# Expert routing: the late tokens of an expert rounded to 64 rows instead of 128, and odd halves of two experts sharing a block

## The chip, the cores and the metric

One core of a Trainium2 chip runs the whole kernel in one launch. The metric is the device time in microseconds (us). TensorE (PE) multiplies, with a weight load (LDWEIGHTS, "PEld") ahead of each matmul; VectorE (DVE), ScalarE (ACT) and GpSimd (POOL) do the elementwise work; SyncE (SP) issues most DMAs, and POOL those that gather or scatter rows by an index.

## The reference, cut to what matters

Attention and a dense mixing layer (with a Fourier transform) make `x`, 8 x 576 = 4608 tokens of 512 channels. The last layer sends every token to one of 8 experts:

```
for b in range(B):
    for s in range(S):
        fresh_e = argmax(x[b, s] @ w_gate)
        e = fresh_e if s == 0 or local_gate[b, s] < 0.5 else prev_e
        prev_e = e
        h = maximum(x[b, s] @ w1[e], 0)          # 512 -> 1024
        out[b, s] = p[e] * (h @ w2[e])           # 1024 -> 512
```

With the inputs of `setup_inputs()` the reference sends 572, 576, 1884, 550, 466, 140, 399 and 21 tokens to experts 0 to 7; of the first four batches' tokens, 572, 0, 772, 9, 455, 125, 371 and 0.

## The kernel before, in words

Attention and the mixing layer take about the first 985 us. The expert stage, which the change touches, works in blocks of 128 tokens of one expert. `place` counts the tokens of each expert and gives each token a row in a block. It runs twice. The early call knows the first four batches only, and fills NEARLY = 9 blocks with whole 128s (four of expert 0, five of expert 2). The late call, when all logits are there, rounds what is left of each expert up to 128 rows: 60, 576, 1244, 550, 466, 140, 399 and 21 tokens make 1, 5, 10, 5, 4, 2, 4 and 1 blocks, 32 in all. Up to 34 are possible; 32 always run (`last_sure`), the last two stand behind branches on the count `used` (`rare`), and are left out with these inputs.

A block b is four steps. `load_x` gathers its 128 rows (POOL's indirect DMA) and turns them with a DMA transpose on SP's queue (xgt: channels on partitions). `e1` makes h: two groups fg of 512 hidden units, each a PSUM tile of 128 x 512 filled by 48 matmuls with a stationary 128x128 piece of w1 and the block's 128 tokens moving (three per pair, since weights and tokens are split in a high and a low f16 half: `PASS`). ACT's relu and one DVE instruction evict each group as the two f16 halves of hx. `e2` takes hx as stationary and w2 as moving operand: 24 matmuls of 512 columns. ACT scales the result (ys), and POOL scatters it to `out`. PE does `e1(b + 1)` before `e2(b)`, so an eviction has an `e2` to hide behind.

The weights of an expert are 2 MB for w1 and 2 MB for w2, each loaded in four pieces of 512 KB. They stand in three slots, and block b uses slot b % 3 (`RB`). `runs` orders the blocks so that those of one slot go through the experts in order, and a slot's expert changes seldom. `weights` issues every piece with a condition (`cond=c`): if the slot already holds the expert, the piece is skipped. A slot's w1 is free again after its own `e1`, and is needed two blocks and an `e2` later. SP issues in order, and each issue waits until the DMA issued eight before it has landed.

A scheduler orders the instructions of each engine, after the order in which they are written. Of two matmul streams that are open it may put pieces of one between pieces of the other. PE runs its list in order.

Of the kernel before, what the change touches and what calls it, by code (L numbers as in the profile page):

```python
# [24 lines left out]
NRARE = 2  # L25
# [4 lines left out]
def runs(n):  # L30

    size = [len(range(r, n, RB)) for r in range(RB)]
    return np.array([s // RB + sum(size[:s % RB]) for s in range(n)])
# [16 lines left out]
def prep(inputs):  # L50
# [105 lines left out]
    c32[:, 607:607 + NBLK - NEARLY] = np.r_[runs(NBLK - NEARLY - NRARE), NBLK - NEARLY - NRARE:NBLK - NEARLY][None, :]  # L156
# [32 lines left out]
def _build(tc, nc, ctx, A, stop):  # L189
# [65 lines left out]
    EB = cp.tile([1, NBLK], F32, name="EB")  # L255
    ebi = cp.tile([1, 2, NBLK], I32, name="ebi")
    used = cp.tile([1, 1], I32, name="used")
# [1039 lines left out]
    def place(nm, ncol, b0, nb, early, rp):  # L1297
# [11 lines left out]
        if ncol < 36:  # L1309
# [8 lines left out]
        nbk = rp.tile([128, 3, 8], F32, tag="nbk", name=f"nbk{nm}")  # L1318
        nc.vector.tensor_scalar(ni, cnt, 0.0 if early else 127.0, None, ALU.add)
        nc.vector.tensor_scalar(ni, ni, 7, None, ALU.arith_shift_right)  # L1320
        nc.vector.tensor_copy(nbk[:, 0], ni)
        nc.vector.tensor_tensor_scan(out=nbk[:, 1], data0=ones[:, 0:8], data1=nbk[:, 0], initial=0.0,
                                     op0=ALU.mult, op1=ALU.add)
        nc.vector.tensor_tensor(nbk[:, 2], nbk[:, 1], nbk[:, 0], op=ALU.subtract)
        if not early:
            nc.vector.tensor_copy(used, nbk[0:1, 1, 7:8])

        cmp = rp.tile([1, NBLK, 8], F32, tag="fs", name=f"cmp{nm}")
        nc.vector.tensor_tensor(cmp[:, :nb], nbk[0:1, 1].unsqueeze(1).to_broadcast([1, nb, 8]),
                                steps[0:1].unsqueeze(2).to_broadcast([1, nb, 8]), op=ALU.is_le)  # L1330
        nc.vector.tensor_reduce(EB[:, b0:b0 + nb], cmp[:, :nb], axis=AX.X, op=ALU.add)
        nc.vector.tensor_scalar(EB[:, b0:b0 + nb], EB[:, b0:b0 + nb], 7.0, None, ALU.min)
        nc.vector.tensor_copy(ebi[:, 0, b0:b0 + nb], EB[:, b0:b0 + nb])
        if b0 == 0:
            nc.vector.memset(ebi[:, 1, 0:RB], 1)
            nc.vector.tensor_tensor(ebi[:, 1, RB:nb], EB[:, RB:nb], EB[:, 0:nb - RB], op=ALU.not_equal)
        else:
            nc.vector.tensor_tensor(ebi[:, 1, b0:b0 + nb], EB[:, b0:b0 + nb], EB[:, b0 - RB:b0 + nb - RB],
                                    op=ALU.not_equal)
# [10 lines left out]
        ob = nbk[:, 2].unsqueeze(1).to_broadcast([128, ncol, 8])  # L1350
        pos = rp.tile([128, 36], F32, tag="pos", name=f"pos{nm}")[:, :ncol]
        if early:
            nc.vector.tensor_tensor(rvn, rvn, oh, op=ALU.mult)
            nc.vector.tensor_reduce(pos, rvn, axis=AX.X, op=ALU.add)
            lim = rp.tile([128, 36], F32, tag="lim", name=f"lim{nm}")[:, :ncol]
            nc.vector.tensor_tensor(rvn, nbk[:, 0].unsqueeze(1).to_broadcast([128, ncol, 8]), oh, op=ALU.mult)
# [102 lines left out]

    def weights(b, dst, src, k0, k1):  # L1460
# [5 lines left out]
        flat = dst[b % RB].rearrange("p c a n -> p (c a n)")  # L1466
        cols = slice(2048 * k0, 2048 * k1)
        nc.sync.dma_start(flat[:, cols], src[bass.ds(e, 1), :, cols].rearrange("o p x -> p (o x)"), cond=c)
# [7 lines left out]
    def e1(b, nxt=None):  # L1476

        ht = M["q"].tile([128, 2, 2, 512], F16, tag="hx", name=f"hx{b}", bufs=3)
        for fg in range(2):
            hp = (psM, psO)[fg].tile([128, 512], F32, tag="ho"[fg], name=f"ehp{b}_{fg}")  # L1480
            for f in range(4):
                n = 0
                cols = slice(128 * f, 128 * f + 128)
                for c in range(4):
                    for (x, y) in PASS:
                        nc.tensor.matmul(hp[:, cols], w1b[b % RB][:, 2 * c + fg, x, cols], xt[b][:, 4 * y + c],  # L1486
                                         start=n == 0, stop=n == 11, skip_group_check=True)
                        n += 1
                if f % 2 == 0 and nxt is not None:
                    load_w1(nxt, 2 * fg + f // 2, 2 * fg + f // 2 + 1)  # L1490
# [7 lines left out]
    def e2(b, nxt=None):  # L1498
        h = hb.pop(b)
        op = psO.tile([128, 512], F32, tag="o", name=f"eo{b}")  # L1500
        n = 0
        for f in range(8):
            for (x, y) in PASS:
                nc.tensor.matmul(op, h[:, f // 4, x, 128 * (f % 4):128 * (f % 4) + 128], w2b[b % RB][:, f, y],  # L1504
                                 start=n == 0, stop=n == 23)
                n += 1
            if f % 2 == 0 and nxt is not None:
                load_w2(nxt, f // 2, f // 2 + 1)
# [68 lines left out]
    e1(0, 2)  # L1577
    last_sure = NBLK - NRARE

    def sure(b):  # L1580
        return b if b < last_sure else None

    for b in range(last_sure):
        if b + RB == NEARLY:
            drain(r1)
        if sure(b + AHEAD) is not None:
            load_x(b + AHEAD)
        if b + 1 < last_sure:
            e1(b + 1, sure(b + RB))
        e2(b, sure(b + RB - 1))  # L1590


    nused = nc.values_load(used, min_val=0, max_val=NBLK - NEARLY)  # L1593

    def rare(b):
        if b == NBLK:
            return
        with tc.If(nused > b - NEARLY):
            load_x(b)
            load_w1(b)  # L1600
            load_w2(b)
            e1(b)
            e2(b)
            rare(b + 1)

    rare(last_sure)
# [17 lines left out]
```

## Time and profile before

| | us |
|---|---|
| three runs: lowest, median, highest | 1441.71, 1446.0, 1447.43 |
| the profiled execution: its time, its span | 1447.72, 1445.9 |
| PE busy | 1390.1 (96%) |
| mean granted TensorE clock | 0.985 |

The profile divides the span in instructions by line, engine and tile. A row with "x96" is 96 like instructions merged, with the first start and the time to the last end; a matmul's own duration holds its way through the array, so what one costs is read from start to start. Names lose their buffer numbers: w1b and w2b are the slots, hx the evicted h, ehp and eo the PSUM tiles of `e1` and `e2`.

### The profile page before, as it was taken

How to read it: one execution, taken by the hardware profiler on the slowest of the kernel's cores; microseconds unless marked ns; L12 is line 12 of the kernel's file. 1: busy time of each engine (PE TensorE's matmuls, PEld its weight loads, DVE VectorE, ACT ScalarE, POOL GpSimd, SP SyncE). 2: the span in 40 equal slices, each digit the busy share in tenths (PEclk: the TensorE clock that was granted, in tenths of full speed). 3: DMA queues.
4: the chain of work that ended last, by engine and by line, in shares of the span. 5: the costliest groups of instructions: out<-in, count | busy, mean ns of one | idle time of the engine just before them, and what ended most of it. 6: DMA issues, size and time to landing. Idle time of an engine off the chain costs nothing. (4 is left out here: it accounts for less than half of the span.)

```text
span 1445.9 us, 28499 instructions
## 1 busy us (share of the span) xinstructions
PE 1390.1 (96%) x11196; PEld 818.5 (57%) x11196; DVE 694.3 (48%) x1397; ACT 518.3 (36%) x953; POOL 382.3 (26%) x392
## 2 busy tenths in 40 slices
PE   7799999999999999999999999998999999999996
PEld 5554455454564544544544566446677776777774
DVE  5899856566625656656657563513821111111110
ACT  2543264455336445545446443111111111111111
POOL 1002243344324334334424332010121121212111
PEclk8999999999999999999999999999999999999998
DMA  6465294764469476476466454526939454962371
GB/s 258 161 221 178 89 261 118 194 202 129 125 162 246 126 191 188 118 194 199 112 184 175 141 132 128 190 68 183 255 82 288 89 145 124 290 202 76 90 237 43
DMA packets 221752, 238.29 MB, mean 165 GB/s; under 512 B 158703, under 2 KB 170095, under 8 KB 218928
## 3 DMA queue, kind: packets, MB, share of 16 engines
q1 hardware_dynamic: 215056, 216.25, 52.7%
q0 software_dynamic: 6560, 20.19, 4.4%
q8 instruction: 89, 1.46, 0.4%
q14 instruction: 47, 0.39, 0.1%
HBM read 268.31 MB, written 53.74 MB: 223 GB/s over the span
## 5 line engine op out<-in xcount | busy, mean ns | idle before, releaser
L1145 PE MATMUL acc<-w,ht 128*128 128x512 f16 x1728 | 409.5, 379 | 0.0
L1125 PE MATMUL hp<-ut,w 128*128 128x512 f16 x1536 | 365.6, 380 | 3.1 <-DMA ut<-unh 2.1
L1125 PEld LDWEIGHTS <-w 128*128 128x128 f16 x1920 | 182.9, 98 | 182.4 <-issue 10.7
L1145 PEld LDWEIGHTS <-ht 128*128 128x128 f16 x1728 | 165.6, 98 | 188.6 <-issue 8.6
L1486 PE MATMUL ehp<-xgt,w1b 128*128 128x128 f16 x3936 | 230.0, 220 | 2.5 <-DMA w1b<-WS 2.5
L1486 PEld LDWEIGHTS <-w1b 128*128 128x128 f16 x3936 | 224.6, 98 | 12.7 <-DMA w1b<-WS 2.8
L333 POOL TENSOR_TENSOR halfs<-stage,halfs 128x512 f16<-128x512 f32 x128 | 151.4, 1188 | 293.9 <-ACT halfs L332 274.5
L1504 PE MATMUL eo<-w2b,hx 128*128 128x512 f16 x984 | 222.2, 382 | 0.0
L1494 DVE SCALAR_TENSOR_TENSOR hx<-ehp,hx 128x512 f16<-128x512 f32 x82 | 56.6, 691 | 330.3 <-ACT hx L1493 330.3
L1133 DVE SCALAR_TENSOR_TENSOR ht<-hp,ht 128x512 f16<-128x512 f32 (+1 forms) x160 | 101.2, 633 | 158.1 <-ACT ht L1132 157.0
L1132 ACT ACTIVATE ht<-hp 128x512 f16<-128x512 f32 (+1 forms) x160 | 88.0, 550 | 231.9 <-PE hp L1125 231.7
L1504 PEld LDWEIGHTS <-hx 128*128 128x128 f16 x984 | 95.0, 98 | 107.2 <-issue 2.7
L1512 POOL DMA_INDIRECT out<-ys,sidx x41 | 42.0, 1023 | 324.0 <-ACT ys L1511 315.8
L1493 ACT ACTIVATE hx<-ehp 128x512 f16<-128x512 f32 x82 | 48.9, 597 | 178.7 <-PE ehp L1486 178.7
L1511 ACT ACTIVATE ys<-eo,scl 128x512 f32<-128x512 f32 x41 | 28.2, 687 | 184.0 <-PE eo L1504 184.0
L332 ACT CAST halfs<-stage 128x512 f16<-128x512 f32 x128 | 77.7, 615 | 9.5 <-DMA WS<-halfs 5.0
L331 ACT ACTIVATE stage<-stage 128x512 f32<-128x512 f32 x128 | 77.7, 623 | 0.2
L1454 POOL DMA_INDIRECT xg<-XS,gidx x41 | 42.4, 1033 | 126.1 <-DVE sidx L1421 50.9
L358 POOL TENSOR_TENSOR qh<-q,qh 128x1420 f16<-128x1420 f32 x12 | 34.6, 2884 | 53.2 <-ACT qh L357 53.1
L1125 PE MATMUL hp<-utr,w 128*128 128x256 f16 x384 | 47.1, 273 | 0.0
L570 PE MATMUL bp<-cst,eh 128*128 128x289 f16 (+1 forms) x168 | 26.2, 291 | 12.8 <-DVE lsum L1166 9.5
L535 POOL TENSOR_TENSOR eo<-ee 128x256 f32<-128x256 f32 (+1 forms) x21 | 17.0, 812 | 76.5 <-DVE ee L519 69.9
(388 smaller groups left out, 1335.2 us busy)
## 6 DMA issues: line engine op xcount, KB each, us to landing
w1b<-WS SPq DMA_DIRECT2D x156, 512.0 KB
w2b<-WS SPq DMA_DIRECT2D x156, 512.0 KB
stage<-in_w SPq DMA_DIRECT2D x64, 512.0 KB
WS<-halfs SPq DMA_DIRECT2D x128, 256.0 KB
q<-in_qd SPq DMA_DIRECT2D x16, 710.0 KB
v<-in_vd SPq DMA_DIRECT2D x16, 640.0 KB
k<-in_kd SPq DMA_DIRECT2D x16, 576.0 KB
XS<-xh SPq DMA_DIRECT2D x36, 256.0 KB
```

The source lines that it names most:

```text
L331: nc.scalar.activation(st[:, a], st[:, a], AF.Copy, scale=64.0 if k < 4 else 256.0)
L332: nc.scalar.copy(so[:, 0], st[:, a])
L333: nc.gpsimd.tensor_tensor(so[:, 1], st[:, a], so[:, 0], op=ALU.subtract)
L1125: nc.tensor.matmul(hp[:, :ntok], w12[:, f, 0, x, 128 * c:128 * c + 128], ut[:, 4 * y + c, :ntok], start=n == 0, stop=n == 11)
L1132: pace[1] = nc.scalar.activation(ht[:, 0, :ntok], hp[:, :ntok], AF.Relu).ins
L1133: pace[0] = nc.vector.scalar_tensor_tensor(ht[:, 1, :ntok], hp[:, :ntok], 0.0, ht[:, 0, :ntok], ALU.max, ALU.subtract).ins
L1145: nc.tensor.matmul(self.acc[j], ht[:, x, 128 * j:128 * j + 128], w12[:, f, 1, y], start=f == 0 and n == 0, stop=f == 15 and n == 2)
L1454: nc.gpsimd.indirect_dma_start(out=g_, out_offset=None, in_=XS[0:rows], in_offset=bass.IndirectOffsetOnAxis(ap=gidx[:, b:b + 1], axis=0), ...
L1486: nc.tensor.matmul(hp[:, cols], w1b[b % RB][:, 2 * c + fg, x, cols], xt[b][:, 4 * y + c], start=n == 0, stop=n == 11, skip_group_check=True)
L1493: nc.scalar.activation(ht[:, fg, 0], hp, AF.Relu)
L1494: nc.vector.scalar_tensor_tensor(ht[:, fg, 1], hp, 0.0, ht[:, fg, 0], ALU.max, ALU.subtract)
L1504: nc.tensor.matmul(op, h[:, f // 4, x, 128 * (f % 4):128 * (f % 4) + 128], w2b[b % RB][:, f, y], start=n == 0, stop=n == 23)
```

## The change: what it does

The late call rounds to 64 rows. An expert with n halves gets n // 2 full blocks and, if n is odd, one half; here 0, 4, 10, 4, 4, 1, 3, 0 full blocks (26) and a half each for experts 0, 1, 3, 5, 6 and 7 (6). A block of pairs holds two halves, rows 0 to 63 of one expert and 64 to 127 of another. 26 full blocks and 3 blocks of pairs always run; up to 4 more full ones stand behind branches on one count, one more block of pairs behind a branch on a second count. So 9 + 26 + 3 = 38 blocks run, where 41 ran.

In `e1_two` tokens are stationary (64 columns) and w1 moves (512 columns), for one half on each side of the array (output partitions 0 to 63 and 64 to 127) from slots 1 and 2. That gives h with tokens on partitions, so `turned` turns it with 16 matmuls against the identity and evicts it again; `e2` does 24 matmuls for each side. The last eight full blocks all use slot 0, and the three blocks of pairs stand between them. `first` and `second` say in which step each weight load is issued. `place` gets some 15 small DVE instructions more.

```diff
+NFULL, NHALF = NBLK - NEARLY - 4, 8
+SFULL, SHALF = 26, 6
+PAIRED = 8
...
+    def place_of(t):
+        if t >= FIRST:
+            return 1 + t % 2 if FIRST % 2 == 0 else 1 + (t + 1) % 2
+        return t % RB if t <= NEARLY + SFULL - PAIRED else 0
...
+    def e1_two(b, todo=()):
+        hh = M["q"].tile([128, 2, 2, 512], F16, tag="hx", name=f"hh{b}", bufs=3)
+        for fg in range(2):
+            hp = (psM, psO)[fg].tile([128, 512], F32, tag="ho"[fg], name=f"ehp{b}_{fg}")
+            n = 0
+            for c in range(4):
+                for (x, y) in PASS:
+                    for a in range(2):
+                        rows = slice(64 * a, 64 * a + 64)
+                        nc.tensor.matmul(hp[rows], xt[b][:, 4 * y + c, rows], w1b[1 + a][:, 2 * c + fg, x],
+                                         start=n == 0, stop=n == 11, skip_group_check=True)
+                    n += 1
...
+            nc.scalar.activation(hh[:, fg, 0], hp, AF.Relu)
+            nc.vector.scalar_tensor_tensor(hh[:, fg, 1], hp, 0.0, hh[:, fg, 0], ALU.max, ALU.subtract)
...
+    def turned(b):
+        hh = hb[b]
+        ht = M["q"].tile([128, 2, 2, 512], F16, tag="hx", name=f"hx{b}", bufs=3)
+        for fg in range(2):
+            for x in range(2):
+                tp = att(f"ht{b}_{fg}_{x}")
+                for f in range(4):
+                    cols = slice(128 * f, 128 * f + 128)
+                    nc.tensor.matmul(tp[:, cols], hh[:, fg, x, cols], idh, start=f == 0, stop=True,
+                                     skip_group_check=True)
+                if x:
+                    nc.vector.tensor_copy(ht[:, fg, x], tp)
+                else:
+                    nc.scalar.copy(ht[:, fg, x], tp)
+                yield
...
     def e2(...)
-                nc.tensor.matmul(op, h[:, f // 4, x, 128 * (f % 4):128 * (f % 4) + 128], w2b[b % RB][:, f, y],
-                                 start=n == 0, stop=n == 23)
+                for a in range(2 if two else 1):
+                    rows = slice(64 * a, 64 * a + 64) if two else slice(0, 128)
+                    c0 = 128 * (f % 4)
+                    nc.tensor.matmul(op[rows], h[:, f // 4, x, c0 + rows.start:c0 + rows.stop], w2b[r + a][:, f, y],
+                                     start=n == 0, stop=n == 23, skip_group_check=True)
...
+    line = list(range(top)) + [top, top + 1, top + 2, FIRST, top + 3, top + 4, FIRST + 1, top + 5, top + 6, FIRST + 2,
+                               top + 7]
+    for t, i in at.items():
+        j = at[before(t)]
+        first.setdefault(("e2", j - 1) if i == j + 1 else ("e1", j + 1), []).append((load_w1, t))
+        second.setdefault(("e1", j + 2) if i == j + 1 else ("e2", j + 1), []).append((load_w2, t))
...
+    nfull = nc.values_load(used[0:1, 0:1], min_val=0, max_val=NFULL)
+    nhalf = nc.values_load(used[0:1, 1:2], min_val=0, max_val=NHALF)
...
+    rare(NEARLY + SFULL)
+    with tc.If(nhalf > SHALF):
+        alone(FIRST + SHALF // 2)
```

The lists of three engines show how the scheduler laid this out. PE before, near the end, where `e1(39)` goes over into `e2(38)` and that into `e1(40)` (ehp39 and ehp40 are outputs of `e1`, eo38 of `e2`):

```order
L1486 MATMUL ehp39_1_16856<-xgt39_16478,w1b0_9398 128x128
L1504 LDWEIGHTS hx38_16645
L1504 MATMUL eo38_16907<-w2b2_10096,hx38_16645 128x512
...
L1504 MATMUL eo38_16907<-w2b2_10096,hx38_16645 128x512
L1486 LDWEIGHTS w1b1_9399
L1486 MATMUL ehp40_0_16942<-xgt40_16643,w1b1_9399 128x128
```

PE after the change, where the first block of pairs (39) ends and the second (40) begins, beside full blocks 31 (`e1`) and 30 (`e2`); "64x512" is a matmul of one side:

```order
L1593 MATMUL eo39_15630<-w2b2_10096,hx39_15432 64x512
L1532 LDWEIGHTS w1b0_9398
L1532 MATMUL ehp31_0_15717<-xgt31_15339,w1b0_9398 128x128
...
L1555 MATMUL ehp40_0_15864<-w1b1_9399,xgt40_15481 64x512
L1593 LDWEIGHTS hx30_15483
L1593 MATMUL eo30_15819<-w2b0_9400,hx30_15483 128x512
...
L1555 LDWEIGHTS xgt40_15481
L1555 MATMUL ehp40_0_15864<-w1b2_10097,xgt40_15481 64x512
```

Before, one step's matmuls stand together; now those of a block of pairs are spread over 27 runs between 128-wide matmuls: 23, 1, 24 and 1, 47 one-sided matmuls for the first block of pairs, and 3, 6, 2, 10, 2, 25 and 3, 2, 10, 2, 31 for each of the other two. The 8 + 8 matmuls of `turned` of blocks 40 and 41 follow their `e1_two` at once.

SP's list after the change, from the load of block 40's w1 on (w1b1 and w1b2 are slots 1 and 2, w1b0 and w2b0 the skipped pieces of full blocks; DMAHW names the landing that an issue waits for):

```order
L1513 DMA w1b2_10097<-WS1_128 128x2048 [waits DMAHW3_49,PE_49]
L1513 ISA
L1513 DMA w1b1_9399<-WS1_128 128x2048 [waits DMAHW4_49,PE_49]
L1513 ISA
L1513 DMA w1b2_10097<-WS1_128 128x2048 [waits DMAHW5_49,PE_49]
...
L1513 DMA w1b0_9398<-WS1_128 128x2048 [waits DMAHW6_49,PE_49]
...
L1491 DMA_TRANSPOSE xgt32_15714<-xg32_15710 128x8x128 [waits DMAHW6_49,DMASW6_49]
...
L1513 DMA w2b1_10095<-WS2_129 128x2048 [waits DMAHW7_49,PE_49]
```

Here two experts' w1 (4 MB) go out together, then skipped pieces and a transpose, then the two w2. Before, one expert's w1 and another's w2 alternate block by block.

POOL's end before, the waits of the way on which the branch isn't taken (ISA adds to the semaphores of the DMAs left out):

```order
L1512 DMA out<-ys_17099,sidx 4608x512 [waits DMASW1_49,DMASW0_49,Activation_49]
L1593 TENSOR_LOAD used [waits DVE_49]
L1598 COMPARE_AND_BRANCH
...
L1598 ISA [waits DMASW4_49,DMASW5_49,DMASW3_49,DMASW2_49]
L1598 UNCONDITIONAL_BRANCH
L1620 ISA [waits barrier_Pool_Activation_PE_DVE_SP_gather]
```

And after the change:

```order
L1604 DMA out<-ys_16701,sidx 4608x512 [waits DMASW2_49,Activation_49]
L1708 TENSOR_LOAD used [waits DVE_49]
L1727 COMPARE_AND_BRANCH
...
L1727 ISA [waits DMASW4_49,DMASW5_49,DMASW3_49,DMASW6_49,DMASW2_49,DMASW7_49,DMASW1_49,DMASW0_49]
L1727 UNCONDITIONAL_BRANCH
L1709 TENSOR_LOAD used
L1732 COMPARE_AND_BRANCH
...
L1732 ISA [waits DMASW5_49,DMASW4_49]
L1732 UNCONDITIONAL_BRANCH
L1747 ISA [waits barrier_Pool_Activation_PE_DVE_SP_gather]
```

There are two of these steps in a row now, and the first waits for all eight semaphores of POOL's DMAs. The last scatter was numbered DMASW1 before, which the ISA didn't wait for; now it is DMASW3, which it does.

## Rows read from the trace of the kernel before

**Rows 1.** The page: the span, and busy time (share) and instructions of PE.
```profile
span 1445.9 us, 28499 instructions
PE 1390.1 (96%) x11196; PEld 818.5 (57%) x11196; DVE 694.3 (48%) x1397; ACT 518.3 (36%) x953; POOL 382.3 (26%) x392
```
**Rows 2.** Waits of PE, 990 to 1100: total us, times, longest.
```profile
PE ehp L1486 <- DMA w1b<-WS: 2.5, 2, 1.4
```
**Rows 3.** Timeline of PE, expert stage: start us, us, engine, line, operation, count.
```profile
1081.67 5.52 PE L1486 MATMUL ehp<-xgt,w1b 128*128 128x128 f16 x96
...
1092.21 5.52 PE L1486 MATMUL ehp<-xgt,w1b 128*128 128x128 f16 x96
...
1408.41 5.52 PE L1486 MATMUL ehp<-xgt,w1b 128*128 128x128 f16 x96
1413.77 5.34 PE L1504 MATMUL eo<-w2b,hx 128*128 128x512 f16 x24
1418.95 5.52 PE L1486 MATMUL ehp<-xgt,w1b 128*128 128x128 f16 x96
1424.31 10.52 PE L1504 MATMUL eo<-w2b,hx 128*128 128x512 f16 x48
```
**Rows 4.** Timeline of PE where attention's two-sided matmuls (128*64) stand.
```profile
216.24 2.11 PE L1125 MATMUL hp<-ut,w 128*128 128x512 f16 x9
218.28 0.84 PE L476 MATMUL gp<-cdt,pth 128*64 128x512 f16 x6
219.05 2.12 PE L1145 MATMUL acc<-w,ht 128*128 128x512 f16 x9
```
**Rows 5.** The same, a longer group.
```profile
80.96 1.03 PE L434 MATMUL pps<-vhl,et 128*64 128x128 f16 x30
81.92 2.33 PE L1125 MATMUL hp<-ut,w 128*128 128x512 f16 x10
```
**Rows 6.** Line 476's weight loads: ns min/median/max, first and last start.
```profile
L476 PEld LDWEIGHTS <-pth x84: 106/109/110, 108.0 to 792.8; 128*64 128x64 f16 x84
```
**Rows 7.** Timeline of ACT and DVE after an `e1`.
```profile
1424.51 0.60 ACT L1493 ACTIVATE hx<-ehp 128x512 f16<-128x512 f32 x1 [1.58 <-PE ehp L1486]
1425.14 0.69 DVE L1494 SCALAR_TENSOR_TENSOR hx<-ehp,hx 128x512 f16<-128x512 f32 x1 [1.49 <-ACT hx L1493]
```
**Rows 8.** Timeline of POOL: a gather behind the late call, the last scatter.
```profile
1052.79 1.03 POOL L1454 DMA_INDIRECT xg<-XS,gidx  x1 [0.98 <-DVE scl L1423]
...
1435.84 0.98 POOL L1512 DMA_INDIRECT out<-ys,sidx  x1 [4.20 <-ACT ys L1511]
```
**Rows 9.** POOL's sequencer in lines 1593, 1598 and 1620: ns min/median/max, first and last start.
```profile
L1593 POOLq TENSOR_LOAD <-used x1: 504/504/504, 1435.6 to 1435.6; - x1
...
L1598 POOLq INC_SWDGE_SEM  x1: 1835/1835/1835, 1436.5 to 1436.5; - x1
...
L1620 POOLq DRAIN  x3: 40/107/6762, 1438.4 to 1445.7; - x3
```
**Rows 10.** Windows of the end: stretch, us, engines' busy time, PEclk, DMA share, GB/s.
```profile
1437.50:1438.00 0.50, 0.00 (x0) 0.00 (x0) 0.00 (x0) 0.00 (x0) 0.00 (x0) 0.50 1.00 385
1438.00:1438.50 0.50, 0.00 (x0) 0.00 (x0) 0.00 (x0) 0.00 (x0) 0.00 (x0) 0.50 0.10 33
```
**Rows 11.** Windows: a stretch with three experts loaded, and one with none.
```profile
1234.00:1288.00 54.00, 54.00 (x618) 39.49 (x616) 6.92 (x10) 9.91 (x16) 10.24 (x10) 1.00 0.97 302
1288.00:1300.00 12.00, 12.00 (x129) 8.35 (x128) 2.07 (x3) 1.97 (x4) 2.05 (x2) 1.00 0.24 68
```
**Rows 12.** SP's queue: four pieces loaded, four pieces skipped.
```profile
1244.82 2.41 SPq L1468 DMA_DIRECT2D w1b<-WS  x4
...
1281.09 1.37 SPq L1468 DMA_DIRECT2D w1b<-WS  x4
```
**Rows 13.** Windows from one expert's w1 load's issue at 1234.28 to its end.
```profile
1240.20:1242.20 2.00, 2.00 (x40) 2.00 (x38) 0.00 (x0) 0.46 (x1) 1.02 (x1) 1.00 1.65 272
1242.20:1244.20 2.00, 2.00 (x40) 2.00 (x38) 0.42 (x1) 0.60 (x1) 1.03 (x1) 1.00 0.58 94
```

More of the change, by code (lines that the diff above doesn't have):

```diff
@@ L24, with runs @@
 NBLK = 43
-NRARE = 2
+NFULL, NHALF = NBLK - NEARLY - 4, 8
+SFULL, SHALF = 26, 6
+NTURN = NEARLY + NFULL + NHALF
+PAIRED = 8
 CW = 650
 RB = 3
-def runs(n):
-    size = [len(range(r, n, RB)) for r in range(RB)]
+def runs(n, extra=0):
+    size = [len(range(r, n, RB)) + extra * (r == 0) for r in range(RB)]
     return np.array([s // RB + sum(size[:s % RB]) for s in range(n)])
@@ L1317, in place @@
         ni = rp.tile([128, 8], I32, tag="ni", name=f"ni{nm}")
[L1318 to L1323, printed above, removed]
@@ new lines, in place @@
+        nc.vector.tensor_copy(nbk[:, 0, 0], ni)
+        if not early:
+            nc.vector.scalar_tensor_tensor(nbk[:, 1, 0], nbk[:, 0, 0], -2.0, nbk[:, 1, 0], ALU.mult, ALU.add)
+        for k in range(kinds):
+            nc.vector.tensor_tensor_scan(out=nbk[:, k, 1], data0=ones[:, 0:8], data1=nbk[:, k, 0], initial=0.0,
+                                         op0=ALU.mult, op1=ALU.add)
+            nc.vector.tensor_tensor(nbk[:, k, 2], nbk[:, k, 1], nbk[:, k, 0], op=ALU.subtract)
+        if not early:
+            nc.vector.tensor_copy(used, nbk[0:1, :, 1, 7])
@@ L1485, in e1 @@
                     for (x, y) in PASS:
-                        nc.tensor.matmul(hp[:, cols], w1b[b % RB][:, 2 * c + fg, x, cols], xt[b][:, 4 * y + c],
+                        nc.tensor.matmul(hp[:, cols], w1b[r][:, 2 * c + fg, x, cols], xt[b][:, 4 * y + c],
                                          start=n == 0, stop=n == 11, skip_group_check=True)
                         n += 1
-                if f % 2 == 0 and nxt is not None:
-                    load_w1(nxt, 2 * fg + f // 2, 2 * fg + f // 2 + 1)
+                if f % 2 == 0:
+                    for fn, t in todo:
+                        fn(t, 2 * fg + f // 2, 2 * fg + f // 2 + 1)
                 if f < 3:
@@ L1503, in e2 @@
             for (x, y) in PASS:
[L1504 to L1508 removed]
+                for a in range(2 if two else 1):
[3 more added lines that the diff above has]
+                                     start=n == 0, stop=n == 23, skip_group_check=True)
+                n += 1
+            if f % 2 == 0:
+                for fn, t in todo:
+                    fn(t, f // 2, f // 2 + 1)
+            if beside is not None and 2 <= f:
+                next(beside, None)
             tick()
@@ L1576, in _build @@
     load_w2(1)
[L1577 to L1584, printed above, removed]
-            drain(r1)
[L1586 to L1593, printed above, removed]
+    top = NEARLY + SFULL - PAIRED
+    line = list(range(top)) + [top, top + 1, top + 2, FIRST, top + 3, top + 4, FIRST + 1, top + 5, top + 6, FIRST + 2,
+                               top + 7]
@@ new lines, in turns @@
+    def turns(b):
+        return [FIRST + 2 * (b - FIRST), FIRST + 2 * (b - FIRST) + 1] if b >= FIRST else [b]
+    at = {t: i for i, b in enumerate(line) for t in turns(b)}
+    first, second = {}, {}
+    for t, i in at.items():
+        if t < RB:
+            continue
+        j = at[before(t)]
+        first.setdefault(("e2", j - 1) if i == j + 1 else ("e1", j + 1), []).append((load_w1, t))
+        second.setdefault(("e1", j + 2) if i == j + 1 else ("e2", j + 1), []).append((load_w2, t))
@@ new lines, in _build, with todo, open_one @@
+    first["e1", 0] = [(load_w1, 2)]
+    second["e2", 0] = [(load_w2, 2)]
+    def todo(kind, i):
+        return first.get((kind, i), []) + second.get((kind, i), [])
+    def open_one(i):
+        b = line[i]
+        (e1_two if b >= FIRST else e1)(b, todo("e1", i))
+    open_one(0)
+    for i, b in enumerate(line):
+        if i + RB == NEARLY:
+            drain(r1)
+        if i + AHEAD < len(line):
+            load_x(line[i + AHEAD])
+        beside = None
+        if i + 1 < len(line):
+            open_one(i + 1)
+            if line[i + 1] >= FIRST:
+                beside = turned(line[i + 1])
+        e2(b, todo("e2", i), beside)
@@ L1595, in rare, with alone @@
+    nfull = nc.values_load(used[0:1, 0:1], min_val=0, max_val=NFULL)
+    nhalf = nc.values_load(used[0:1, 1:2], min_val=0, max_val=NHALF)
+    def alone(b):
+        load_x(b)
+        for t in turns(b):
+            load_w1(t)
+            load_w2(t)
+        if b >= FIRST:
+            e1_two(b)
+            for _ in turned(b):
+                pass
+        else:
+            e1(b)
+        e2(b)
     def rare(b):
-        if b == NBLK:
+        if b == NEARLY + NFULL:
             return
[L1598 to L1603, printed above, removed]
+        with tc.If(nfull > b - NEARLY):
+            alone(b)
```

82 lines of the change are left out of this document (60 added, 22 removed).

## The prediction

> **What bounds the kernel now.** I read the page first: PE is busy in 96% of the span, every other engine in less than half of it, PE's weight loads apart, which lie beside its matmuls [rows 1]. Then the waits of PE in the expert stage: between 990 and 1100 us the weights cost it 2.5 us [rows 2], and later than that the list of its waits is empty. Then PE's timeline: from 1092.21 to the end each block takes 5.36 us for `e1` (start 1408.41 to start 1413.77) and 5.18 us for `e2` (to 1418.95), the same at the first late blocks (1081.67 to 1092.21 is one block) and at the last [rows 3]. So one late block costs PE 10.54 us, a 128-column matmul 5.36 / 96 = 0.0558 us and a 512-column one 5.18 / 24 = 0.2158 us. Nothing but the number of matmul columns sets this stage. Work taken from PE there comes off the time one for one until something else is late; work added there is paid in full. After PE's last matmul come ACT's scaling, a scatter, a branch and the drain: the tail.
>
> **The blocks.** The late tokens (60, 576, 1244, 550, 466, 140, 399, 21) make 32 blocks before; after, 26 full blocks and three of pairs. So six blocks of 10.54 us go, 63.24 us, and three blocks of pairs come.
>
> **A block of pairs on PE.** It has 48 one-sided matmuls in each of `e1_two` and `e2`, 96 in all, 288 for the three blocks. If both sides run at once, that is 144 times 0.2158; in PE's list some stand without a partner before the next 128-wide matmul, and I count 150 slots: 32.37 us. Do both sides run at once? Attention shows it: line 476 issues six 512-column matmuls of one side each, and from its first start (218.28) to the next line's (219.05) are 0.77 us [rows 4]. Three slots are 0.65, six would be 1.29. With 30 short ones it is 0.96 us for 15 slots worth 0.84 [rows 5]. Their weight loads, 109 ns for each one-sided matmul [rows 6], leave no trace in this. The excess is 0.12 us in both, whether three pairs or fifteen, so it is paid per group and not per matmul. At the group's entry the nine matmuls ahead take 2.04 us (216.24 to 218.28) in place of 9 x 0.2158 = 1.94, another 0.10. I take 0.22 us for each run of one-sided matmuls, 0.10 to 0.30 as bounds.
>
> What speaks against the change is the scheduler's list: it spreads the 288 over 27 runs between 128-wide matmuls. 27 x 0.216 = 5.83 us; written as three blocks in one piece it would be under 1.5. The Trainium skill has this rule too ("TensorEngine Tiling (Array Packing)", Tiling Modes, Key Properties): a change of the tiling mode drains TensorE; it names no price. By that rule each of the 27 runs pays twice, which is how the rows were read; without it the sum below would be 5.8 us lower.
>
> **Turning.** 16 matmuls of 128 columns per block of pairs: 48 x 0.0558 = 2.68 us. They also bring a wait. In the lists of blocks 40 and 41 they stand right behind `e1_two`, with nothing between. ACT's relu starts 0.20 us after the last matmul (1424.31 to 1424.51), takes 0.60, DVE then 0.69 [rows 3, 7]: 1.49 us until the second half's low part is there; its PSUM tile is free after one more eviction (0.69), and four transposes follow (0.22): about 2.45 us, in which PE has 16 x 0.0558 = 0.9 of its own. So 1.55 us stall in each of two blocks, 3.1; block 39's stand between matmuls of an `e2` and wait for nothing. Bounds: 0 (PE's queue has something else after all) and 2.45 each, 4.9.
>
> **PE's sum.** -63.24 + 32.37 + 5.83 + 2.68 + 3.1 = -19.26 us.
>
> **The tail.** Before, the last scatter is issued at 1435.84 [rows 8]. POOL's sequencer reads `used` in 0.50 us, runs the not-taken branch, whose semaphore addition starts at 1436.5 and takes 1.84, and a drain of 6.76 ends the launch [rows 9]. This addition doesn't wait for the last scatter, whose data moves until shortly before 1438.5 [rows 10]. After the change it waits for all eight semaphores, the last scatter's too, so it starts up to 2.0 us later; behind it are a second read (0.50), branch (0.05) and addition (1.84): 2.4 more. Nothing of PE is left to cover this, so +4.5. Bounds: 0 (the drain waits for something that ends at the same moment anyway) and 4.5. I take 4.5, since each piece has a row of its own.
>
> **The routing.** The late `place` gets some 15 small DVE instructions, about 3 us. The gather that waits for its table is issued at 1052.79 [rows 8], and the `e1` of that block starts at 1081.67 [rows 3]: 28.9 us of cover. Nothing; without the cover 3 us.
>
> **Weights.** Pieces that the slot already holds are quick on SP, four in 1.37 us against 2.41 for four that move [rows 12], and nothing waits behind them. With three experts loaded one behind the other the DMAs moved 302 GB/s at a busy share of 0.97, and PE, busy 54.00 of 54.00 us, waited for none, at a granted clock of 1.00 [rows 11]. The pairs need more at once: two experts, 4 x 2.1 = 8.4 MB, and rows for three blocks at 0.72 MB each (68 GB/s x 12 us over 1.14 blocks [rows 11]), 10.5 MB from one block of pairs to the next. At 302 GB/s that is 34.9 us. One period is two full blocks (21.1), a block of pairs (10.8 + 0.9), nine switches (2.0) and a stall (1.6): 36.4. It fits with 1.5 us to spare. I cost it at nothing; as a rival it has its price.
>
> **Sum.** -19.26 + 4.5 = -14.8 us. The profiled execution took 1447.7, so 1432.9; it lies 1.7 above the median of 1446.0, so 1431 for the median. Own range, with switches at 0.10 to 0.30 (-3.1, +2.3), stalls 0 to 4.9 (-3.1, +1.8) and the tail 0 to 4.5 (-4.5, 0): all at once 1420 to 1435; not all go one way, and slots that I miscounted go upwards: 1424 to 1437.
>
> **Rivals.**
>
> *The pairs' weights come late.* For it: only 1.5 us to spare, w1 of both sides (4 MB) goes out together and w2 of both behind it, and one expert's w1, issued at 1234.28, took until about 1243 when alone [rows 13], so 8.8 us for 2 MB. Against: the same traffic for 54 us without a wait [rows 11]. At 280 GB/s the period would be 37.5, 1.1 us too long, and an order in which w2 or a gather stands behind the wrong piece costs half a load, 4.4 us, once or twice. +1 to +9, some +6: 1437. The rows' switch gaps would stand beside PE waits for w1b or w2b.
>
> *The two sides take turns.* This one makes it slower. Place: every one-sided matmul of the three blocks. If the two sides, with two different weights moving and a weight load each, do not overlap, the 288 take 62.15 us in place of 32.37: +29.8, so 1461. It decides from the point where more than about half of the pairs run in turn. Against it: [rows 4, 5], two lines that overlap completely, with 109 ns of weight load per one-sided matmul [rows 6] beside them. For it: these lines' runs are short, so 24 pairs on end with evictions beside them aren't shown. The Trainium skill ("TensorE: Matmul & The Clock Gate", Part 3, What overlaps and what doesn't) says that a weight load overlaps matmuls under way only if its row group differs, and both sides here have the same rows; taken alone that would lay bare 288 loads of 0.109 us, 31 us, and give 1462. The trace doesn't agree: six such loads are 0.65 us, and with three slots laid end to end they would be 1.3, where 0.77 was measured [rows 4].
>
> *A branch is taken*, so the change doesn't do what it says with these inputs. Expert 1's 576 tokens are exactly nine halves; a token more there, by rounding of the logits, makes ten, one full block too many, and the 27th stands alone behind a branch, with nothing to hide it: load of w1 8.8 us [rows 13], `e1` and `e2` 10.54, evictions and scatter about 4: +23.5, so 1455. For it: only the count; against: the counts of the other experts are 4 or more tokens off a border, and before no branch was taken: the addition is that of the way not taken [rows 9].
>
> **Chances.** Forecast 0.80, late weights 0.12, a branch 0.05, sides in turn 0.03. About 0.5% (7.2 us) is what a measurement of this kernel can tell from no change. Faster by more means under 1438.8: nearly all of the forecast (0.77 of 0.80), and two thirds of the late weights (0.08): 0.85. Within 0.5%, 1438.8 to 1453.2: what is left of both, and a branch that is cheaper than worked out: 0.08. Slower: 0.07. Range for 8 in 10: 1424 below, and above 1440, which takes in most of the late weights.
>
> **What would show it.** The profile after should have 38 gathers and scatters where 41 were, PE 19 us less in the late stage, 0.1 us more than 0.2158 at every change between 128-wide and one-sided matmuls and none inside a run, two stalls of about 1.5 us before the turning matmuls of blocks 40 and 41 put down to ACT or DVE, no wait of PE for a weight, and two semaphore additions in POOL's tail with the end some 4.5 us later behind the last scatter than before. One-sided matmuls that start 0.2158 apart singly rather than in pairs, waits on w1b or w2b in the last 110 us, or a 39th block would make it wrong.

## The result

| us | before | after |
|---|---|---|
| median (lowest to highest) | 1446.72 (1441.71 to 1452.7, 4 runs) | 1427.26 (1423.79 to 1432.05, 4 runs) |
| the profiled execution: time, span | 1447.72, 1445.9 | 1428.91, 1427.1 |

The ratio is 0.9866 (95% interval 0.9817 to 0.9915). 1431 was forecast, 0.9896 of 1446.0; a later, longer comparison (below) gave 0.9912 (0.9887 to 0.9937), so the forecast lies between the two and inside both intervals. One execution of the kernel together (below), at 1770.19 us and a granted clock of 0.748, was slow and is in no number here. How much of the profiled 18.8 us is the change is best read in three pieces: what lies ahead of the first undisturbed `e1` (head), from there to ACT's last scaling (stage), and from there to the end of the span (tail).

| us | head | stage | tail |
|---|---|---|---|
| before | 1060.59 | 374.28 | 11.03 |
| after | 1056.92 | 355.01 | 15.17 |
| difference | -3.67 | -19.27 | +4.14 |

The page of the profile after, span and PE (before: [rows 1]):

```profile
span 1427.1 us, 27701 instructions
PE 1367.0 (96%) x10812; PEld 788.0 (55%) x10812; DVE 695.5 (49%) x1412; ACT 516.3 (36%) x950; POOL 389.1 (27%) x386
```

The waits of PE from 990 to 1430 us (total, times, longest), two short ones left out; before, [rows 2] and the gate's wait:

```profile
PE lp L1166 <- DMA xt<-xh: 4.4, 2, 4.0
PE ht L1573 <- ACT hx L1578: 1.2, 2, 0.6
PE ht L1573 <- DVE hh L1562: 0.8, 2, 0.4
PE tabf L1419 <- DVE stage L1430: 0.8, 1, 0.8
...
PE ehp L1532 <- DMA w1b<-WS: 0.4, 1, 0.4
```

There is no wait for a weight after 1031 us, and the two waits before `ht`, the turning, are new. PE's timeline, after, at the blocks of pairs (start, us, operation, count; 128*64 is one side; compare [rows 3 to 5]):

```profile
1056.92 5.52 PE L1532 MATMUL ehp<-xgt,w1b 128*128 128x128 f16 x96
...
1299.76 2.78 PE L1555 MATMUL ehp<-w1b,xgt 128*64 128x512 f16 x23
1302.47 0.51 PE L1532 MATMUL ehp<-xgt,w1b 128*128 128x128 f16 x6
1302.91 0.40 PE L1555 MATMUL ehp<-w1b,xgt 128*64 128x512 f16 x1
1303.25 4.86 PE L1532 MATMUL ehp<-xgt,w1b 128*128 128x128 f16 x84
...
1347.74 2.99 PE L1555 MATMUL ehp<-w1b,xgt 128*64 128x512 f16 x25
1350.67 0.62 PE L1573 MATMUL ht<-c,hh 128*128 128x128 f16 x8
1351.89 0.38 PE L1573 MATMUL ht<-c,hh 128*128 128x128 f16 x4 [0.61 <-ACT hx L1578]
1352.67 0.40 PE L1573 MATMUL ht<-c,hh 128*128 128x128 f16 x4 [0.39 <-DVE hh L1562]
1352.90 0.33 PE L1532 MATMUL ehp<-xgt,w1b 128*128 128x128 f16 x3
```

Read it from start to start. 23 one-sided matmuls, 12 slots of 0.2158 = 2.59, take 2.71 until the next line begins: the two sides run at once, and the way out costs 0.12. A single one takes 0.34, again 0.12 over its slot. Ahead of it, six short matmuls (0.335) take 0.44: the way in, 0.10. Every run of one-sided matmuls pays both, whatever its length: the runs of 2, 3, 6, 10 and 25 between 1333.8 and 1350.7 take 0.12 over their slots too. The turning takes 2.23 us (1350.67 to 1352.90) for 0.89 of work, a stall of 1.34.

POOL's sequencer in the tail (ns min/median/max, first and last start; before: [rows 9]; the last scatter is now issued at 1412.89):

```profile
L1708 POOLq TENSOR_LOAD <-used x1: 507/507/507, 1412.7 to 1412.7; - x1
...
L1727 POOLq EVENT_SEMAPHORE  x4: 17/43/2285, 1413.4 to 1415.9; - x4
...
L1727 POOLq INC_SWDGE_SEM  x1: 1699/1699/1699, 1416.0 to 1416.0; - x1
...
L1709 POOLq TENSOR_LOAD <-used x1: 313/313/313, 1417.7 to 1417.7; - x1
...
L1732 POOLq INC_SWDGE_SEM  x1: 1679/1679/1679, 1418.3 to 1418.3; - x1
...
L1747 POOLq DRAIN  x3: 40/107/6272, 1420.0 to 1426.9; - x3
```

The wait for the last scatter's semaphore (2.29 us) and the second read and addition (0.31 and 1.68) are there one behind the other.

### The profile page after: what moved, and what is told of

Its sections match the earlier page's. It is cut to its first block, busy times and chain, and to the rows that moved or that the text cites. A ratio compares the mean times of both kernels' runs of the same rounds, so it can differ in the third digit from the quotient of the medians.

```text
span 1427.1 us, 27701 instructions
## 1 busy us (share of the span) xinstructions
PE 1367.0 (96%) x10812; PEld 788.0 (55%) x10812; DVE 695.5 (49%) x1412; ACT 516.3 (36%) x950; POOL 389.1 (27%) x386
## 5 line engine op out<-in xcount | busy, mean ns | idle before, releaser
L1129 PEld LDWEIGHTS <-w 128*128 128x128 f16 x1920 | 183.0, 98 | 182.5 <-issue 11.7
L1593 PE MATMUL eo<-w2b,hx 128*128 128x512 f16 (+1 forms) x984 | 210.1, 381 | 0.0
L1532 PE MATMUL ehp<-xgt,w1b 128*128 128x128 f16 x3360 | 199.3, 219 | 0.4 <-DMA w1b<-WS 0.4
L1532 PEld LDWEIGHTS <-w1b 128*128 128x128 f16 x3360 | 191.6, 98 | 13.4 <-issue 3.5
L1541 DVE SCALAR_TENSOR_TENSOR hx<-ehp,hx 128x512 f16<-128x512 f32 x70 | 48.3, 691 | 294.7 <-ACT hx L1540 294.7
L1593 PEld LDWEIGHTS <-hx 128*128 128x128 f16 (+1 forms) x984 | 87.5, 100 | 99.4 <-issue 7.5
L1604 POOL DMA_INDIRECT out<-ys,sidx x38 | 38.7, 1018 | 279.9 <-ACT ys L1603 279.6
L1540 ACT ACTIVATE hx<-ehp 128x512 f16<-128x512 f32 x70 | 41.8, 597 | 162.7 <-PE ehp L1532 162.5
L1487 POOL DMA_INDIRECT xg<-XS,gidx x38 | 52.5, 1380 | 141.6 <-DVE sidx L1454 51.5
```

The lines of the kernel that those rows point to most:

```text
L1129: nc.tensor.matmul(hp[:, :ntok], w12[:, f, 0, x, 128 * c:128 * c + 128], ut[:, 4 * y + c, :ntok], start=n == 0, stop=n == 11)
L1487: nc.gpsimd.indirect_dma_start(out=g_, out_offset=None, in_=XS[0:rows], in_offset=bass.IndirectOffsetOnAxis(ap=gidx[:, b:b + 1], axis=0), ...
L1532: nc.tensor.matmul(hp[:, cols], w1b[r][:, 2 * c + fg, x, cols], xt[b][:, 4 * y + c], start=n == 0, stop=n == 11, skip_group_check=True)
L1540: nc.scalar.activation(ht[:, fg, 0], hp, AF.Relu)
L1541: nc.vector.scalar_tensor_tensor(ht[:, fg, 1], hp, 0.0, ht[:, fg, 0], ALU.max, ALU.subtract)
L1593: nc.tensor.matmul(op[rows], h[:, f // 4, x, c0 + rows.start:c0 + rows.stop], w2b[r + a][:, f, y], start=n == 0, stop=n == 23, skip_group_ ...
```

## Experiments

Stage and tail are the pieces of the table above, read from one profile of each kernel. The ratio is to the kernel before, with its 95% interval.

| kernel | median, us | ratio | stage | tail |
|---|---|---|---|---|
| again (changed kernel) | 1431.64 | 0.9912 (0.9887 to 0.9937) | 355.02 | 15.33 |
| onecount | 1429.55 | 0.9904 (0.9880 to 0.9928) | 355.01 | 12.67 |
| nobranch | 1427.02 | 0.9860 (0.9824 to 0.9896) | 355.02 | 9.04 |
| written | 1468.71 | 1.0164 (1.0135 to 1.0192) | 392.40 | 15.0 |
| written2 | 1442.15 | 0.9977 (0.9960 to 0.9994) | 367.24 | 15.0 |
| atonce2 | 1443.10 | 0.9989 (0.9967 to 1.0011) | 369.22 | 15.1 |
| best | 1440.53 | 0.9981 (0.9960 to 1.0002) | 364.59 | 12.7 |
| apart | 1454.67 | 1.0064 (1.0041 to 1.0086) | 374.33 | 15.0 |
| together | 1432.55 | 0.9889 (0.9857 to 0.9922) | 357.17 | 15.64 |
| both | 1430.15 | 0.9890 (0.9861 to 0.9920) | 353.14 | 13.34 |
| spaced | 1433.66 | 0.9910 (0.9884 to 0.9936) | 355.00 | 16.29 |

### again: what is chance

The changed kernel, unedited.

> The changed kernel once more. The late stage (first undisturbed e1 to last e2) took 354.8 us against 374.1 before, -19.3, the tail 14.2 against 10.1, +4.2: together -15.1. The rest of the profiled difference of 18.8 us lies ahead of that stage, from 982 to 1057 us, 3.7 us in all (a shorter wait for w1b, a shorter wait for xt, and an e2 at full clock). Theory A: those 3.7 us are chance of two executions; the ratio is 0.9896 and this profile shows other waits there. Rival B: they belong to the change (the late loads and the routing are issued otherwise); the ratio is 0.987 and the first undisturbed e1 starts within 0.5 us of 1056.9 again.

The ratio is theory A's: 0.9896 lies in its interval, B's 0.987 below it. This profile alone decides less: its waits ahead of the stage are like those of the first (3.9 us for `xt` in both), and its first undisturbed `e1` starts at 1057.45, 0.53 us from 1056.92, where B said within 0.5. The stage came out at 355.02 us, within 0.01 of the first profile, and again in two further kernels that don't touch it. What speaks for A is that the head varies: 1053.42 (onecount) to 1063.52 us (apart) in the profiles of kernels whose head is the same code but for an instruction. The one profile of the kernel before, 1060.59, lies inside that spread. One cause of the spread can be seen. PE stands for the gate's `xt`, and the `e2` behind that wait runs at full clock or at half. Windows of PE's wait and of what follows, first the kernel before (us, busy time of PE, PEld, DVE, ACT, POOL, then PEclk):

```profile
993.00:998.00 5.00, 0.27 (x5) 0.10 (x2) 0.00 (x0) 0.00 (x0) 0.00 (x0) 0.87 0.73 202
998.80:1003.00 4.20, 4.20 (x13) 1.54 (x11) 1.60 (x4) 1.37 (x3) 0.00 (x0) 0.50 0.98 225
```

and then onecount (below), in the same place:

```profile
992.30:994.00 1.70, 0.02 (x1) 0.00 (x0) 0.00 (x0) 0.00 (x0) 0.00 (x0) 1.00 0.92 270
994.50:998.90 4.40, 4.40 (x23) 1.82 (x20) 1.78 (x4) 1.32 (x2) 0.00 (x0) 1.00 1.20 265
```

Behind a wait of 4.9 us the granted clock was 0.50 (1.2 of 2.4 GHz), behind one of 1.7 it stayed at 1.00. The `tabf` matmuls of the longer `place` waited 0.4 to 1.4 us for DVE in most of these profiles, but not where w1b came later still (written); so the routing, costed at nothing, costs at most that.

### written, atonce, written2: the switches taken out, and what came instead

written: from two blocks ahead of the first pair the steps run in the order in which they are written, so the one-sided matmuls stand in 6 runs.

```diff
+        if i == line.index(FIRST) - 2:
+            written.enter_context(tc.manual_schedule())
...
```

> The last steps, from two blocks ahead of the first pair on, in the order in which they are written: one-sided matmuls in 6 runs in place of 27, 144 slots in place of 150, turning matmuls between an e2's. Theory A (each run of one-sided matmuls costs 0.22 us for going in and out, whatever its length; the stalls of 1.34 us before two turnings go): 21 x 0.22 + 6 x 0.2158 + 2 x 1.34 = 8.6 us less than the changed kernel, and the three blocks of pairs 35.3 us in place of 44.0. Rival B (the excess goes by the matmul, not by the run): 4.0 less, from stalls and slots alone. Rival C: the written order brings waits for weights or evictions that the scheduler's order avoids; no faster, with PE waits in the list.

Rival C, which had said no faster: it is 37 us slower than the changed kernel. PE's waits from 1280 us on, then POOL's and SP's timelines:

```profile
PE ehp L1532 <- DMA w1b<-WS: 25.4, 11, 7.5
PE eo L1593 <- DMA w2b<-WS: 9.0, 2, 4.7
```

```profile
1319.05 0.98 POOL L1604 DMA_INDIRECT out<-ys,sidx  x1 [17.90 <-ACT ys L1603]
1320.34 1.05 POOL L1487 DMA_INDIRECT xg<-XS,gidx  x1 [0.30 <-issue]
```

```profile
1306.49 2.53 SPq L1513 DMA_DIRECT2D w2b<-WS  x5
1323.67 1.27 SPq L1491 DMA_TRANSPOSE xgt<-xg  x1
1327.03 0.08 SPq L1513 DMA_DIRECT2D w1b<-WS  x1
```

Nothing is issued between 1309.0 and 1323.67, and from 1310 to 1323 the DMAs were busy 0.18 of the time. The transpose waits for a gather (1320.34), which stands in POOL's queue behind a scatter (1319.05) that waits for an `e2`; the weights stand behind the transpose. The scheduler's order had the gather ahead of that scatter.

atonce was meant to be the same with the turning at once behind `e1_two`. The turning matmuls were in fact left out of it (its blocks of pairs pass h unturned), so it tells nothing on the stall; its 1466.62 us (1.0163) repeat the waits of written.

> As the kernel in written order, but the 16 turning matmuls of each of the three blocks of pairs come at once behind e1_two, with nothing between. Theory A: PE stands 1.3 to 1.5 us in each, waiting for ACT and DVE: 3 x 1.4 = 4.2 us more than in the written order, so some 4.5 less than the changed kernel. Rival: the weight loads or e2's own matmuls fill the wait, and the two orders take the same time within 1 us.

written2 takes that cause away: each gather and transpose is issued one block earlier.

```diff
...
+        if own and i + AHEAD + 1 < len(line):
+            load_x(line[i + AHEAD + 1])
         e2(b, todo("e2", i), beside)
```

> Written order again (one-sided matmuls in 6 runs), but each block's gather and transpose are issued a block earlier, ahead of the e2 and the scatter that they stood behind. In the first written order PE waited 36.7 us for weights; SP's queue stood at transposes (1309 to 1323.7, 1329.9 to 1341.4) that waited for a gather behind a scatter, with the weights behind them. Theory A: that was the cause; the waits for weights go, and the sum of switches, slots and stalls comes out: the three blocks of pairs cost 35.3 us in place of 44.0, the time is 8.6 less than the changed kernel's. Rival B: the loads wait because a skipped piece stands behind eight real ones in SP's queue; then w1b waits of some us remain before the full blocks and it is no faster than the changed kernel. Rival C: the DMAs can't bring 8.4 MB of weights and the rows of three blocks in a period of 32.8 us; the busy share is near 1 and the waits are for pairs' weights.

A was the larger part: 25 of the 37 us went. What stayed has the look of rival B, waits for w1b before full blocks and no gain over the changed kernel, but not its cause. PE's timeline, then SP's, POOL's and what SP waited for between 1320 and 1346:

```profile
1316.77 5.37 PE L1555 MATMUL ehp<-w1b,xgt 128*64 128x512 f16 x48
1322.07 2.12 PE L1593 MATMUL eo<-w2b,hx 128*128 128x512 f16 x9
...
1333.61 5.37 PE L1593 MATMUL eo<-w2b,hx 128*64 128x512 f16 x48
1342.16 0.34 PE L1532 MATMUL ehp<-xgt,w1b 128*128 128x128 f16 x3 [3.18 <-DMA w1b<-WS]
...
1344.94 7.61 PE L1532 MATMUL ehp<-xgt,w1b 128*128 128x128 f16 x87 [0.32 <-DMA w1b<-WS]
1352.39 5.34 PE L1593 MATMUL eo<-w2b,hx 128*128 128x512 f16 x24
```

```profile
1326.16 6.50 SPq L1513 DMA_DIRECT2D w1b<-WS  x8
1338.66 1.27 SPq L1491 DMA_TRANSPOSE xgt<-xg  x1
1342.04 0.09 SPq L1513 DMA_DIRECT2D w1b<-WS  x1
```

```profile
1330.63 1.04 POOL L1487 DMA_INDIRECT xg<-XS,gidx  x1 [0.30 <-issue]
```

```profile
SPq L1491 <- DMA xg<-XS,gidx: 11.7, 2, 5.9
```

The `e1` of a full block starts at 1342.16, right behind a piece of w1b issued at 1342.04 in 0.09 us: a skipped piece. It moves nothing, but its turn in SP's queue comes only when the transpose ahead has gone, at 1338.66. The transpose stood 5.9 us, and not for the eight real pieces issued from 1326.16 on but for its gather: issued at 1330.63, while those pieces were moving, the gather landed only at 1338.64, 8.0 us later, where the one before it (1319.14) took 3.6. The second wait of this kind is alike (issued at 1371.52, landed at 1379.71). Behind the transpose SP needs another 2.1 us, in which it reads the block's expert and condition, before the skipped piece. And the wait is paid twice in this profile: the 87 matmuls behind it take 7.45 us for 4.85, the granted clock in 1345 to 1352 being 0.61, so part of them ran at the lower of its two levels (1.2 GHz). The switches themselves did what was said: 48 one-sided matmuls in one run take 5.30 us (1316.77 to 1322.07), 24 x 0.2158 + 0.12, the same 0.12 as for a single one.

### atonce2, apart: the stall, and the two sides

atonce2 is written2 with the turning at once behind `e1_two` (`for _ in turned(line[i + 1]): pass`).

> As written2, with the 16 turning matmuls of each block of pairs at once behind its e1_two. Theory A: PE stands 1.3 to 1.5 us in each, 4.2 us more than written2 in all, with waits of ht for ACT and DVE in the list. Rival: no difference over 1 us.

```profile
PE ehp L1532 <- DMA w1b<-WS: 11.9, 11, 3.9
PE ht L1573 <- ACT hx L1578: 1.9, 3, 0.6
PE ht L1573 <- DVE hx L1576: 1.4, 3, 0.5
```

The waits of `ht` are there in each block, 1.4 us over its work (1318.56 to 1320.89 is 2.33 for 0.89), 4.3 in the three, as A said. The stage is only 2.0 longer, and the times can't be told apart, but the stalls were not covered by later waits: those for w1b are 11.9 us here and 12.3 in written2. What differs is the clock. In written2 the 87 matmuls from 1305.00 on take 6.49 us at a granted clock of 0.74, here the same ones, behind the same three waits (0.56, 0.77 and 1.08), take 4.86 at 1.00. The kernel best (below), which has written2's late order, ran that stretch at 1.00 too, and its stage is 2.65 shorter than written2's; against best the stage of atonce2 is 4.6 longer. So in these orders a stage is not repeated to better than some 2.7 us.

apart is written2 with all of one side ahead of all of the other in each group (the loop over `a` outside those over `c` and `f`; the points at which weight pieces are issued move with it).

> As written2, but the matmuls of a block of pairs go side by side in time: in each group all of one side first, then all of the other, so that no two neighbours in PE's list use different sides. Theory A (neighbours of different sides run at once, in turn they don't): 144 slots become 288, 29 to 30 us more than written2. Rival (the sides take turns in any case, or the engine pairs them across the order): within 3 us of written2.

```profile
1319.51 8.05 PE L1555 MATMUL ehp<-w1b,xgt 128*64 128x512 f16 x48
1327.49 2.12 PE L1592 MATMUL eo<-w2b,hx 128*128 128x512 f16 x9
...
1339.03 9.71 PE L1592 MATMUL eo<-w2b,hx 128*64 128x512 f16 x48
1348.68 0.51 PE L1532 MATMUL ehp<-xgt,w1b 128*128 128x128 f16 x6
```

Neither theory's number. `e1_two` takes 7.98 us in place of 5.30 and `e2` 9.65 in place of 5.37, 6.96 more per block; wholly in turn each would be 10.36, and 0.12 for the way out. What is missing from this 10.48 is 0.83 in `e2`, with one border between the sides, and 2.50 in `e1_two`, with three: 0.83 us at each border. The starts show the same: at each border four matmuls of the one side and four of the other start in pairs, at most 0.03 us apart, and all others stand some 0.2 apart. Of the 20.9 us that PE lost only 7.1 are seen in the stage, because the waits for weights fell from 12.3 to 5.6 us and no lowered clock followed them, which had cost written2 6.6. That the sides overlap as neighbours is shown; that PE loses 30 without it is not.

### onecount, nobranch: the tail

onecount puts both conditions into one (`most` is the larger of the full count and the half count + 20):

```diff
+    with tc.If(most > SFULL):
+        nfull = nc.values_load(used[0:1, 0:1], min_val=0, max_val=NFULL)
+        nhalf = nc.values_load(used[0:1, 1:2], min_val=0, max_val=NHALF)
         rare(NEARLY + SFULL)
```

> The two conditions behind the last block become one (DVE works out the larger of the two counts; what was there stands inside its branch, not taken). Theory A (the steps of POOL's tail stand one behind the other, each with its own price): the second read 0.31, its branch and its semaphore addition 1.68 go, 2.1 us less than the changed kernel, and the time from the last scatter's issue to the end falls from 14.2 to 12.1. Rival: the drain of 6.3 us ends at a time of its own, and the end doesn't move: 0.

> The changed kernel without its branches (they aren't taken with these inputs; counts that need them aren't served). Theory A (the tail's steps add up, the drain runs behind them): the reads 0.5 + 0.3, the wait for the last scatter's semaphore 2.3 and the additions 1.7 + 1.7 go, but the drain may itself wait for the scatter's data: between 4 and 6.5 us less than the changed kernel, from the last scatter's issue to the end 8 to 10 us in place of 14.2. Rival (the drain ends at its own time): 14 us stay.

The tail fell from 15.17 and 15.33 to 12.67 with one condition, 2.5 to 2.7 us; the times' intervals overlap, so this rests on the profile. Without branches it is 9.04. There the drain starts at once behind the last scatter and takes longer (nobranch; the changed kernel's row stands above):

```profile
L1741 POOLq DRAIN  x3: 40/107/7495, 1415.8 to 1423.8; - x3
```

By these two profiles the drain takes in part of the wait for the scatter (7.50 against 6.27), not all of it: A in the main. From the last scatter's issue to the end are 8.1 us, 8 to 10 were expected.

### best, together, both, spaced: a faster version?

best is written2 with onecount's condition. It kept the waits for weights, 11.7 us.

> written2 and one condition behind the last block in place of two. Theory A: the gains add up: 8.6 + 2.3 = 10.9 us less than the changed kernel, ratio to before some 0.983. Rival: the weights' waits remain and only the 2.3 of the tail are seen.

together leaves the scheduler its order of SP's queue and only raises the priority of the one-sided matmuls, those of `e2` likewise:

```diff
+                        with tc.high_priority(offset=200):
                             nc.tensor.matmul(hp[rows], xt[b][:, 4 * y + c, rows], w1b[1 + a][:, 2 * c + fg, x],
...
```

> The scheduler keeps the order of SP's queue of the changed kernel; only the one-sided matmuls get a higher priority, which puts them in 11 runs in place of 27, all of even length (144 slots in place of 150), and the turning matmuls behind 20 matmuls of an e2. Theory A (each run costs 0.22 us, each odd end a slot of 0.2158, each turning at once behind e1_two 1.3): 16 x 0.22 + 6 x 0.2158 + 2 x 1.3 = 7.4 us less than the changed kernel, less some 1 us of waits for PSUM at the turnings, so 6.5 less, with no wait for weights. Rival (the loads set the pace as in the two written orders): waits for w1b or w2b of 3 us and more, no faster than the changed kernel.

> The higher priority of the one-sided matmuls and the single condition behind the last block. Theory A: 6.5 + 2.3 = 8.8 us less than the changed kernel; the ratio to the kernel before some 0.983, the lowest of all. Rival: waits for weights eat the first part, 2.3 less.

The rival, in part. The waits of PE in together from 1280 us on, its timeline at the third block of pairs, and SP's queue ahead of it:

```profile
PE ehp L1556 <- DMA w1b<-WS: 3.7, 3, 2.5
...
PE ehp L1532 <- DMA w1b<-WS: 1.0, 1, 1.0
```

```profile
1340.46 0.51 PE L1532 MATMUL ehp<-xgt,w1b 128*128 128x128 f16 x6
...
1373.90 0.81 PE L1556 MATMUL ehp<-w1b,xgt 128*64 128x512 f16 x5 [2.53 <-DMA w1b<-WS]
```

```profile
1343.58 7.85 SPq L1491 DMA_TRANSPOSE xgt<-xg  x1
1353.00 0.09 SPq L1513 DMA_DIRECT2D w1b<-WS  x1
...
1359.90 9.19 SPq L1513 DMA_DIRECT2D w1b<-WS  x9
```

The second block's `e1_two` has left slots 1 and 2 at 1340.46; their next w1 is issued 19 us later, behind a transpose of 7.85 and four pairs of skipped pieces, and PE, whose order is now shorter, comes for it before it has landed. The stage was 2.2 us longer than the changed kernel's in together and 1.9 shorter in both, which has the same late order but for its condition. So no gain is shown: of the 4.0 us between these two, 2.0 are longer waits for w1b and 1.6 a stretch at a lowered clock behind them in together (0.71 in 1376.26 to 1382.21, 1.00 at the same matmuls in both).

spaced lets three full blocks stand between blocks of pairs, so that a period is longer.

> As the kernel with the higher priority and the single condition, but three full blocks instead of two stand between the first and the second and between the second and the third block of pairs (one list of block numbers is changed; the last block of pairs now comes last). A period is then some 43 us for the same weights. Theory A (the waits for w1b of 4.8 us, and the lowered clock behind them, come from a period too short for its loads): they go, and the sum of runs, slots and stalls is seen: 14 runs in place of 27, 144 slots, so the stretch from the first undisturbed e1 to the last scaling takes 349 us in place of 355.0, and with the single condition the time is 8.4 us less than the changed kernel's. Rival B (the loads wait for SP's queue whatever the period): w1b waits of 3 us and more stay, and the stretch takes 353 us or more.

Rival B, but for its 3 us of waits for w1b: the waits for weights after 1280 us fell to 2.8 us but didn't go, with a period of 45 us (1292.66 to 1337.95) and the DMAs busy 0.80 of it. Each wait for w1b ends right behind a skipped piece: these are issued at 1337.68, 1343.23 and 1388.67, and PE goes on 0.11 to 0.12 us later. So it is the place in SP's queue that sets them. The stage was 355.00, no better. And the last two `e2` end together, so that their scatters queue: they are issued at 1414.59 and 1419.12, and the tail grew to 16.3.

Stage and tail together are 370.2 us in the changed kernel, 367.7 in onecount and 366.5 in both. Both is the shortest that keeps the branches, 3.7 less by one profile, of which 1.9 is stage that together didn't repeat; by the times (0.9890 against 0.9912, overlapping intervals) it isn't shown to be faster. nobranch is lowest, but serves only such counts.

## Why the prediction was right

By its own steps:

- **The blocks.** 38 blocks ran, no branch was taken.
- **PE's sum**, -19.26: the stage moved by -19.27. The terms one by one: both sides at once, shown by the timeline and by apart; switches 0.22 a run, 5.8 in all, as in [rows 4, 5]; the stall 1.34 twice, where 1.55 was said; 0.16 before block 39's turning, where nothing was said. The agreement to 0.01 is luck: the stalls came 0.4 lower than the sum has them, and as much was spent elsewhere, 0.16 of it at block 39 and the rest not assigned.
- **The tail**, +4.5: +4.14. The wait was 2.29 where 2.0 was said, each addition 1.7 where 1.84 was, the second read 0.31 where 0.50 was; the drain 6.27 where 6.76 was. Here too errors offset one another: the named pieces make 3.7, small steps of POOL's sequencer between them the other 0.4.
- **Weights.** No wait, as said. From the second block's turning to the third's (1350.67 to 1387.25) are 36.58 us, 36.4 was worked out; in them the DMAs moved 263 GB/s, 9.6 MB, at a busy share of 0.75. The period before it was tighter: in 1314 to 1351 they moved 291 GB/s, 10.8 MB, where 10.5 was worked out, at a share of 0.92. So the rate had some room in both. What the prediction left out is the order of SP's queue: the runs that shortened PE's list all met waits for weights, and written, with 37 us, shows what an order can cost that puts a gather behind a scatter, where this rival had said 4.4 us once or twice.
- **The size.** -14.8 was forecast; the profiled pair showed -18.8, since its heads differ by 3.67. The heads of like kernels differ by 10 us, so this part can't be put down to the change; the longer comparison gave 1445.11 to 1431.64, -13.5.
- **Sides in turn.** Not so. That rival's price was not met either: apart, which takes the sides apart but for four pairs a border, lost 20.9 on PE, not 29.8.

The 27 runs, which the prediction held against the change at 5.8 us, do cost that; yet putting the matmuls together is not shown to gain: the stage was 2.2 us longer in one such kernel and 1.9 shorter in the other, since most of what PE saved came back as waits for weights and lowered clock.

## To carry to other kernels

Read the price of a rare kind of instruction from start to start at its neighbours, where the same kind stands elsewhere in the trace, and ask whether it goes by instruction or by run; two small groups of attention priced the 27 switches to 0.1 us. Before tightening the order of the busiest engine, look at what the in-order DMA queue puts ahead of its loads: a transpose behind a gather behind a scatter, or a skipped load that still takes its turn, can cost more than the order saves. Compare profiles piece by piece with a landmark between, since a head that varies by 10 us hides a stage that repeats to 0.01. Ask of each stage whether it repeats: with waits in it, and the clock behind them, two of the same order differed by 2.65 and by 4.0 us.

## What was not expected of the hardware

- A skipped DMA is not free: in written2 PE waited 3.2 and 4.0 us for pieces that move nothing, because they stood behind a transpose that waited for its gather.
- A gather issued beside eight weight pieces of 512 KB took 8.0 and 8.2 us to land in written2; the one at 1319.14 took 3.6.
- A wait of PE of 3.2 us and shorter ones behind it were followed by a granted clock of 0.61 over 7 us in written2 (2.6 us lost), the gate's wait of 4.9 by 0.50 (the level of 1.2 GHz). The same waits need not do the same: behind waits of 0.56, 0.77 and 1.08 us the granted clock was 0.74 in written2 (1.6 us lost) and 1.00 (2.4 GHz) in atonce2 and apart.
- When a whole side is written first, one-sided matmuls of different sides overlap only at the border, four of each, 0.83 us (apart).
